# Hash attention and a maxout FFN on one core: order of the first hash, units of the values' parts, distance of the v loads, unit of one scaling, and two banks for the last product

## The chip, the cores and the metric

The kernel runs on one core of one Trainium2 chip. The metric is the device time of the whole program in microseconds (us). Three runs of the kernel before gave 295.3, 296.67 and 298.35 us; the median is 296.67 us. One execution was profiled, and all profile lines come from it.

## The reference

For 4 batches and 8 heads, `q`, `k` and `v` have 768 rows of 64 numbers. Each row of `q` and of `k` is projected on 6 directions, and the 6 signs give a bucket number. A query sees only the keys of its own bucket:

```
mask   = q_bucket[:, :, :, None] == k_bucket[:, :, None, :]
scores = 0.125 * q @ k.T ;  scores = where(mask, scores, -1e9)
attn   = softmax(scores) ;  a = attn @ v
x      = a.transpose(0, 2, 1, 3).reshape(3072, 512)
h      = max(x @ w1, x @ w2, x @ w3)          # w1..w3: 512 x 768
out    = h @ w_out                            # w_out: 768 x 512
```

Inputs and output are float32.

## The kernel before, in words

**Pairs and units.** The work is cut into 16 pairs of heads (4 per batch). A pair has 12 units: two query halves of 384 columns, times three pairs of key blocks, times two heads. So there are 192 units, 48 per batch, and u = 12 * pair + place. In this text "unit n" is the pass of the main loop (L408) with u = n, and its "slot" is u % 6. The scores of unit u+1 are issued in the pass of unit u.

**One unit.** `scores(u)` (L296) makes two matmuls of 384 columns into a double bank `sc` (two such buffers), and ScalarE takes the exponential of all 768 columns into one of 14 tiles `AT` (L304). The 70 rows that are contracted are 64 of the head and 6 of the hash, at +0.5 or -0.5, so that equal buckets add up to a constant that the bias takes away again; unequal buckets fall far below and vanish in the exponential.

**Values.** `values_part` (L316) multiplies the AT tiles of two units with the values `vo` into the bank `av`, four products side by side on 32 columns of the array each, and with ones into `sm`, the row sums. A query half has three parts. The last part comes in the pass after the half's last unit, in `values` (L336), where VectorE also moves `av` and `sm` out as `avs` and `ys` (L343 to L346). There is one `av` bank, so the first part of the next half needs `avs` to be done. The first two parts lie in slots 2 and 4 (L441). Pair 0's first half and pair 1's first half get all three parts at once.

**Preparation.** For each pair `prep_groups` (L133) yields four transposes groups `tgroup` (L143: three transposes into a bank `mp` of the pool `ms`, then VectorE copies to `T2` and, for pairs 2 to 7, to the odd half of `S`) and one `hashes` (L200: four float32 products side by side, VectorE turns them into `bits`, and four small DMAs put the bits into `S`). `even` (L216) is a GpSimd copy into `S`. One of these is issued in each "fill" slot: 1, 3 and 5 until unit 60, then 1 and 4 (L432). Preparation runs up to 6 pairs ahead. The pool `ms` has three banks; it also serves `sm`, the hash and the FFN.

**The start.** Pair 0 goes by a list written out by hand (L223 to L230). In it k and q of head 0 and k of head 1 are transposed first (L226), then the hash of head 0 runs (`hash_first`, L181: per head and side two float32 products, one per query or key half `par`, in different 32 columns), then q of head 1 is transposed. `bits_first` (L194) writes the signs straight into `S`, in pieces of (side, par, columns). For the first half of pair 0 and pair 1 the units of head 0 come ahead of those of head 1 (L284), so unit 3 is the first that needs head 1.

**Normalising.** `normalize` (L352) sends `ys` by DMA to 32 rows (`dd`), VectorE adds and inverts them (`rr`), a DMA writes them to DRAM (`rd`), and two DMAs spread them over 64 rows each (`rb`). GpSimd then multiplies `avs` and `rb` into `xT` (L381). A batch's last pair does that for each query half with the steps 7, 11 and 15 units after the half's end (L386); the others once per pair.

**FFN.** The groups of batch b-1 (L234) join the stream from place 13 of batch b on, so the first is due at unit 61 (`FFN_AT`, L291). They take turns with the units by a credit of 0.66 per unit. A first layer group is four matmuls of 384 columns, the fourth of which reads what the batch's last pair gave. A second layer product is six matmuls of 512 columns into one bank; ScalarE copies it out and a DMA of the sync queue stores it. The very last one is copied half by ScalarE and half by VectorE (L268 to L272).

**Queues.** All order is the order of the source (`manual_schedule`, L390): each engine works off its own list in order. GpSimd's list holds the casts of v (L125), the even copies, the scalings and also the issuing of nearly all loads: q and k (L115), v (L122), weights (L418) and bits (L214). `load_v` for pair p+1 is issued at the first unit of pair p (L411), its cast at place 10 (L415). The sync queue issues `dd`, `rd`, `rb` and the output.

Of the kernel before, what the change touches and what calls it, by code (L numbers as in the profile page):

```python
# [9 lines left out]
FP32 = mybir.dt.float32  # L10
# [7 lines left out]
def kernel(  # L18
# [114 lines left out]
    def prep_groups(pi):  # L133
# [34 lines left out]
                        nc.vector.tensor_copy(o, i_)  # L168
            return go

        def odd_first(hd):
            for side in (1, 0):
                o, i_ = st["S"][0:D, side, hd, 1, :], st["T2"][D : 2 * D, side, hd, :]
                if hd == 0:
                    nc.scalar.copy(o, i_)
                else:
                    nc.vector.tensor_copy(o, i_)

        first_bp = {}

        def hash_first(hd, sides=(1, 0)):  # L181
            for side in sides:
                if hd == 1:
                    bp = ms_ps.tile([P, 512], FP32, tag="ms", name="bp")
                elif side == 1:
                    bp = sc_ps.tile([P, 2, 512], FP32, tag="sc", name="bp0")[:, 0]
                else:
                    bp = av_ps.tile([P, 512], FP32, tag="av", name="bp1")
                first_bp[side, hd] = bp
                for par in range(2):  # L190
                    nc.tensor.matmul(bp[32 * par : 32 * par + 32, 0:HALF], pj[:, 1 + par, :], st["T2"][:, side, hd, :],  # L191
                                     start=True, stop=True)

        def bits_first(hd, parts):  # L194
            for side, par, lo, hi in parts:
                nc.vector.tensor_scalar(out=st["S"][D:KR, side, hd, par, lo:hi],
                                        in0=first_bp[side, hd][32 * par : 32 * par + NBITS, lo:hi],
                                        scalar1=0.0, scalar2=0.5, op0=AluOp.is_gt, op1=AluOp.subtract)
# [22 lines left out]
            return lambda: copy(st["S"][0:D, side, :, 1, :], st["T2"][D : 2 * D, side])  # L221

        if pi == 0:  # L223
            k0, k1 = (1, 0, 0, P), (1, 1, 0, P)
            early = (k0, k1, (0, 0, 0, HALF), (1, 0, P, HALF), (1, 1, P, HALF))
            return [tgroup(1, 0), tgroup(0, 0), tgroup(1, 1), lambda: odd_first(0), lambda: hash_first(0), tgroup(0, 1),  # L226
                    lambda: bits_first(0, early), lambda: scores(0), lambda: hash_first(1, (1,)), lambda: odd_first(1),
                    lambda: bits_first(1, early[:2]), lambda: scores(1), lambda: scores(2), lambda: hash_first(1, (0,)),
                    lambda: bits_first(1, early[2:]), lambda: bits_first(0, ((0, 1, 0, HALF),)),
                    lambda: bits_first(1, ((0, 1, 0, HALF),))]  # L230
        odds = [odd(1), odd(0)]
        return [tgroup(s, h) for h in (0, 1) for s in (1, 0)], hashes, [even], odds if pi == ODD_LATE or pi >= ODD_PSUM else []

    def ffn_groups(b):  # L234
        xb = xts[b]
        gs = []
        for hf in range(2):
            hts = {}
            for fb in range(NFB):
                for wi in range(3):  # L240
                    def go(fb=fb, wi=wi, hf=hf, hts=hts):
                        ps = ms_ps.tile([P, 512], FP32, tag="ms", name="l1")
                        for jc in range(NJC):
                            nc.tensor.matmul(ps[:, 0:HALF], w_sb[wi][:, jc, fb * P : (fb + 1) * P],  # L244
                                             xb[:, jc, hf * HALF : (hf + 1) * HALF],
                                             start=(jc == 0), stop=(jc == NJC - 1))
                        if wi == 0:
                            hts[fb] = hpool.tile([P, HALF], FP16, tag="ht", name="ht")
                            nc.vector.tensor_copy(hts[fb][:], ps[:, 0:HALF])  # L249
                        else:  # L250
                            nc.vector.tensor_tensor(out=hts[fb][:], in0=hts[fb][:], in1=ps[:, 0:HALF], op=AluOp.max)  # L251
                    gs.append((0.66, go, 0))
            for tb in range(CH2):
                st2 = {}

                def part(f0, f1, tb=tb, hts=hts, st2=st2):
                    if f0 == 0:
                        st2["l2"] = ms_ps.tile([P, 512], FP32, tag="ms", name="l2")
                    for fb in range(f0, f1):
                        nc.tensor.matmul(st2["l2"][:, 0:DM], hts[fb][:, tb * P : (tb + 1) * P], wout_sb[:, fb, :],  # L260
                                         start=(fb == 0), stop=(fb == NFB - 1))
                    return st2["l2"]

                def go2(tb=tb, hf=hf, part=part):
                    ps = part(NFB // 2, NFB)
                    osb = opool.tile([P, DM], FP32, tag="osb", name="osb")
                    rows = out[b * S : (b + 1) * S, :].rearrange("(p c) m -> p c m", c=NCH)
                    if (b, hf, tb) == (B - 1, 1, CH2 - 1):  # L268
                        nc.scalar.copy(osb[:, 0 : DM // 2], ps[:, 0 : DM // 2])
                        nc.vector.tensor_copy(osb[:, DM // 2 :], ps[:, DM // 2 : DM])  # L270
                        nc.scalar.dma_start(rows[:, 2 * tb + hf, 0 : DM // 2], osb[:, 0 : DM // 2])
                        nc.sync.dma_start(rows[:, 2 * tb + hf, DM // 2 :], osb[:, DM // 2 :])  # L272
                    else:
                        nc.scalar.copy(osb[:], ps[:, 0:DM])  # L274
                        nc.sync.dma_start(rows[:, 2 * tb + hf, :], osb[:])
                gs += [(0.66, lambda part=part: part(0, NFB // 2), 0), (0.66, go2, 0)]
        return gs


# [72 lines left out]
    def normalize(pi, q0, nq):  # L352

        b, jj = divmod(pi, HPAIR)
        if jj == 0:
            xts[b] = xpool.tile([P, NJC, S], FP16, tag="xT", name="xT")
        xt, avs, ys = xts[b], avs_of[pi], ys_of[pi]
        G = 16
        W = nq * HALF // G
        dd = small.tile([2 * G, 2, 2 * HALF // G], FP32, tag="dd", name="dd")  # L360
        rr = small.tile([2 * G, 2 * HALF // G], FP32, tag="rr", name="rr")
        rd = drp.tile([2 * G, W], FP32, tag=f"rd{nq}", name="rd")
        rb = rbpool.tile([P, 2, HALF], FP32, tag="rb", name="rb")

        def gather():
            for half in range(2):
                nc.sync.dma_start(dd[:, half, 0:W], ys[32 * half : P : D, q0 : q0 + nq, :])

        def invert():
            nc.vector.tensor_reduce(rr[:, 0:W], dd[:, :, 0:W].rearrange("p h w -> p w h"), axis=mybir.AxisListType.X,  # L370
                                    op=AluOp.add)
            nc.vector.reciprocal(rr[:, 0:W], rr[:, 0:W])  # L372
            nc.sync.dma_start(rd[:, :], rr[:, 0:W])

        def spread():
            for hd in range(2):
                nc.sync.dma_start(rb[hd * D : (hd + 1) * D, 0:nq, :],
                                    rd[hd * G : (hd + 1) * G, :].rearrange("(o p) i -> o (p i)", o=1).to_broadcast((D, nq * HALF)))

        def scale(i):  # L380
            return lambda: nc.gpsimd.tensor_mul(xt[:, jj, (q0 + i) * HALF : (q0 + i + 1) * HALF],  # L381
                                                avs[:, q0 + i, :], rb[:, i, :])
# [113 lines left out]
```

## Time and profile before

| what | value |
|---|---|
| median of three runs | 296.67 us (295.3 to 298.35) |
| the profiled execution's own time | 295.93 us |
| its span, first to last instruction | 294.0 us |
| granted TensorE clock, mean | 0.998 |
| TensorE busy (matmul) | 285.0 us, 97% |
| VectorE, ScalarE, GpSimd busy | 188.7, 195.4, 139.7 us |
| start of the first exponential | 9.08 us |
| first FFN group's last matmul starts | 71.05 us |
| end of the last matmul | 290.07 us |

The span is 1.93 us shorter than the time of the same execution; that rest lies outside of the instructions. Busy shares of TensorE hide short waits, since a matmul's row lasts until its result has left the array and so overlaps the next one. The starts of the rows, and their distance, tell more than the shares.

### The profile page before, as it was taken

The page shows a single profiled execution, that of the slowest core. Times are in us where ns is not written, and L with a number is a line of the kernel's source. Part 1 is how long each engine was busy: PE and PEld are TensorE (multiplying, and loading weights), DVE is VectorE, ACT ScalarE, POOL GpSimd, SP SyncE. Part 2 cuts the span into 40 slices and gives each one's busy share as a digit, 9 for nine tenths or more (in the row PEclk, how much of TensorE's full clock was granted, in tenths as well). Part 3 has the DMA queues.
Part 4 walks back from the last instruction along what each step waited for, and adds up shares of the span by engine and source line. Part 5 has one row for each costly group of instructions (what it writes and reads, how often), then busy time and mean ns, then how long its engine had stood idle before and what let it go on. Part 6 is the DMA issues. An engine that isn't in the chain of part 4 may idle for free.

```text
span 294.0 us, 6792 instructions
## 1 busy us (share of the span) xinstructions
PE 285.0 (97%) x2592; PEld 159.7 (54%) x2592; DVE 188.7 (64%) x419; ACT 195.4 (66%) x238; POOL 139.7 (48%) x187
## 2 busy tenths in 40 slices
PE   8898999998999999999999999999999999999994
PEld 4454454444656566555665556555655555555551
DVE  2886977788865387736667377654757167657480
ACT  3779899886847956797785965888696956010202
POOL 2765799889806556291905636090801702220000
PEclk9999999999999999999999999999999999999999
DMA  6877666864952733336222522315011211230203
GB/s 206 266 166 204 164 169 186 233 161 123 271 158 63 233 97 116 107 67 261 83 88 64 176 107 59 101 48 175 9 54 59 102 49 41 64 134 2 107 0 108
DMA packets 20276, 35.90 MB, mean 122 GB/s; under 512 B 6080, under 2 KB 12484, under 8 KB 20244
## 3 DMA queue, kind: packets, MB, share of 16 engines
q0 software_dynamic: 8992, 19.81, 25.2%
q1 hardware_dynamic: 10948, 15.52, 16.3%
q8 instruction: 20, 0.33, 0.5%
q10 hardware_dynamic: 304, 0.13, 0.2%
q14 instruction: 12, 0.10, 0.1%
HBM read 31.46 MB, written 6.39 MB: 129 GB/s over the span
## 4 chain that ended last, share of the span: by engine, by line
PE 90%; DMA 3%; DVE 2%; ACT 2%; issue 1%; POOL 0%; SPq 0%; ACTq 0%; POOLq 0%; DVEq 0%
PE l L244 32%; PE sc L301 21%; PE av L327 11%; PE l L260 11%; PE mp L150 6%; PE sm L332 5%; PE bp L205 3%; DMA rb<-rd 2%; ACT AT L304 2%; PE wm L393 1%; PE bp L191 1%; DMA rd<-rr 0%; DVE S L168 0%; POOL xT L381 0%; DVE rr L372 0%
## 5 line engine op out<-in xcount | busy, mean ns | idle before, releaser
L304 ACT ACTIVATE AT<-sc,bias_t 128x768 f16<-128x768 f32 x192 | 168.9, 903 | 53.9 <-PE sc L301 48.3
L244 PE MATMUL l<-xT,w_sb 128*128 128x384 f16 x576 | 110.0, 326 | 1.0 <-POOL xT L381 1.0
L301 PE MATMUL sc<-S 70*128 70x384 bf16 x384 | 93.8, 327 | 1.8 <-ACT AT L304 1.5
L244 PEld LDWEIGHTS <-w_sb 128*128 128x128 f16 x576 | 55.9, 97 | 36.3 <-issue 1.5
L214 POOL DMA_DIRECT2D S<-bits x58 | 32.9, 570 | 86.0 <-DVE bits L208 55.5
L251 DVE TENSOR_TENSOR ht<-ht,l 128x384 f16<-128x384 f16 x96 | 52.9, 551 | 18.1 <-PE l L244 13.5
L301 PEld LDWEIGHTS <-S 70*128 70x128 bf16 x384 | 33.8, 98 | 41.7 <-issue 20.2
L327 PE MATMUL av<-AT,vo 128*32 128x385 f16 x768 | 48.3, 330 | 1.0 <-DVE avs L344 0.7
L381 POOL TENSOR_TENSOR xT<-avs,rb 128x384 f16<-128x384 f32 x32 | 31.5, 1000 | 31.1 <-DMA rb<-rd 31.1
L249 DVE CAST ht<-l 128x384 f16<-128x384 f32 x48 | 26.5, 553 | 25.3 <-PE l L244 24.4
L274 ACT COPY osb<-l 128x512 f32<-128x512 f32 x23 | 13.4, 585 | 35.0 <-PE l L260 35.0
L260 PE MATMUL l<-wout_sb,ht 128*128 128x512 f16 x144 | 36.5, 379 | 0.0
L332 PE MATMUL sm<-AT,ones 128*32 128x384 f16 x384 | 32.7, 324 | 0.0
L327 PEld LDWEIGHTS <-vo 128*32 128x32 f16 x768 | 17.3, 95 | 20.0 <-issue 10.9
L160 DVE COPY T<-mp 128x384 f32<-128x384 f32 x31 | 17.0, 549 | 13.7 <-PE mp L150 13.6
L158 DVE TENSOR_SCALAR T<-mp 128x384 f32<-128x384 f32 x30 | 16.6, 554 | 12.7 <-PE mp L150 11.3
L217 POOL CAST S<-T 64x1536 bf16<-64x1536 f32 x15 | 22.1, 1476 | 0.0
L260 PEld LDWEIGHTS <-ht 128*128 128x128 f16 x144 | 14.0, 97 | 12.7 <-DVE ht L251 0.2
L344 DVE TENSOR_SCALAR avs<-av,sv 128x384 f32<-128x384 f32 x32 | 19.8, 618 | 1.6
L346 DVE TENSOR_SCALAR ys<-sm 128x384 f32<-128x384 f32 x32 | 17.5, 548 | 0.0
L343 DVE TENSOR_SCALAR sv<-av 128x1 f32<-128x1 f32 x32 | 5.1, 158 | 18.3 <-PE av L327 17.8
L150 PE MATMUL mp<-iden,knat 128*128 128x128 f32 x96 | 16.2, 277 | 0.0
(45 smaller groups left out, 191.4 us busy)
## 6 DMA issues: line engine op xcount, KB each, us to landing
out_dram<-osb SPq DMA_DIRECT2D x23, 256.0 KB
vnat<-in_v_dram POOLq DMA_DIRECT2D x15, 384.0 KB, 4.8
knat<-in_k_dram POOLq DMA_DIRECT2D x13, 384.0 KB, 4.3
qnat<-in_q_dram POOLq DMA_DIRECT2D x13, 384.0 KB, 5.1
rb<-rd SPq DMA_DIRECT2D x24, 192.0 KB
w_sb<-in_moe_w_dram POOLq DMA_DIRECT2D x12, 192.0 KB, 4.7
rb<-rd SPq DMA_DIRECT2D x16, 96.0 KB
S<-bits POOLq DMA_DIRECT2D x58, 9.0 KB, 2.4
```

Of the source, the lines that this page charges most:

```text
L150: nc.tensor.transpose(mp[:, i * P : (i + 1) * P], n[:, hd, 2 * i * D : (2 * i + 2) * D], iden[:])
L214: eng.dma_start(st["S"][D:KR, side, hd, :, :], bits[p0 : p0 + 2 * NBITS, :])
L217: nc.gpsimd.tensor_copy(st["S"][0:D, :, :, 0, :], st["T2"][0:D])
L244: nc.tensor.matmul(ps[:, 0:HALF], w_sb[wi][:, jc, fb * P : (fb + 1) * P], xb[:, jc, hf * HALF : (hf + 1) * HALF], start=(jc == 0), stop=(j ...
L249: nc.vector.tensor_copy(hts[fb][:], ps[:, 0:HALF])
L251: nc.vector.tensor_tensor(out=hts[fb][:], in0=hts[fb][:], in1=ps[:, 0:HALF], op=AluOp.max)
L260: nc.tensor.matmul(st2["l2"][:, 0:DM], hts[fb][:, tb * P : (tb + 1) * P], wout_sb[:, fb, :], start=(fb == 0), stop=(fb == NFB - 1))
L301: nc.tensor.matmul(sc[:, j, 0:HALF], th[0:KR, 1, hd, j, kp * P : (kp + 1) * P], th[0:KR, 0, hd, qh, :], start=True, stop=True)
L304: nc.scalar.activation(at[:, :, 0:HALF], sc[:, :, 0:HALF], ActFn.Exp, bias=bias_t[:], scale=SCALE)
L327: nc.tensor.matmul(av[p0 : p0 + 32, 0 : HALF + 1], vones[pi][:, hd, d0 : d0 + 32], ats[hd][:, c % 2, 0 : HALF + 1], start=(c == 0), stop=( ...
L332: nc.tensor.matmul(sm[32 * t : 32 * t + 32, 0:HALF], ones[:, :], ats[hd][:, half, 0:HALF], start=(s == 0), stop=(s == CH2 - 1))
L381: return lambda: nc.gpsimd.tensor_mul(xt[:, jj, (q0 + i) * HALF : (q0 + i + 1) * HALF], avs[:, q0 + i, :], rb[:, i, :])
```

## The change

It has five parts.

1. **The first hash in pieces.** `odd_first` and `hash_first` take single sides and single pieces. Head 0's list is now: transposes of k and q; the products of k's first 128 columns (both halves), of q's first half; their bits; the products of k's other 256 columns; transposes of head 1's k; scores 0; head 1's k products; then transposes of head 1's q; scores 1; the product of head 1's first q half; scores 2; and last the products of the second q halves of both heads, one by one.
2. **Parts and fills.** Until unit 60 the fills are in slots 1, 2 and 4 and the values' parts in slots 3 and 5 (the third stays in slot 0).
3. **v.** Pair p+2's v is loaded from place 8 of pair p on (pair 1's from unit 0), and cast at place 4 of the pair before its own (pair 1's at unit 10 still).
4. **Scaling.** The scaling of a batch's last pair, except the very last pair, comes 14 units after a half's end in place of 15.
5. **The last product** is computed in two halves of 256 columns, each with six matmuls into a bank of its own. VectorE copies the first and the sync queue stores it, ScalarE copies the second and its own queue stores it. It is one FFN item instead of two.

```
-        def odd_first(hd):
+        def odd_first(hd, side):
+            copy = nc.scalar.copy if hd == 0 else nc.vector.tensor_copy
+            copy(st["S"][0:D, side, hd, 1, :], st["T2"][D : 2 * D, side, hd, :])
...
+        def hash_first(hd, parts):
+            for side, par, lo, hi in parts:
+                if (side, hd) not in first_bp:
...
+                nc.tensor.matmul(first_bp[side, hd][32 * par : 32 * par + 32, lo:hi], pj[:, 1 + par, :],
+                                 st["T2"][:, side, hd, lo:hi], start=True, stop=True)
...
-            k0, k1 = (1, 0, 0, P), (1, 1, 0, P)
-            early = (k0, k1, (0, 0, 0, HALF), (1, 0, P, HALF), (1, 1, P, HALF))
-            return [tgroup(1, 0), tgroup(0, 0), tgroup(1, 1), lambda: odd_first(0), lambda: hash_first(0), tgroup(0, 1),
...
+            ka, kb = [[(1, par, lo, hi) for par in range(2)] for lo, hi in ((0, P), (P, HALF))]
+            qa, qb = [[(0, par, 0, HALF)] for par in range(2)]
+            hf, bf = hash_first, bits_first
+            return [tgroup(1, 0), tgroup(0, 0), lambda: odd_first(0, 1), lambda: odd_first(0, 0),
+                    lambda: hf(0, ka), lambda: hf(0, qa), lambda: bf(0, ka), lambda: bf(0, qa),
+                    lambda: hf(0, kb), tgroup(1, 1), lambda: bf(0, kb), lambda: scores(0),
+                    lambda: hf(1, ka + kb), lambda: odd_first(1, 1), lambda: bf(1, ka), tgroup(0, 1),
+                    lambda: scores(1), lambda: hf(1, qa), lambda: odd_first(1, 0), lambda: bf(1, qa), lambda: scores(2),
+                    lambda: bf(1, kb), lambda: hf(1, qb), lambda: hf(0, qb), lambda: bf(0, qb), lambda: bf(1, qb)]
...
+                    if last:
+                        for c0, copy, eng in ((0, nc.vector.tensor_copy, nc.sync), (DM // 2, nc.scalar.copy, nc.scalar)):
+                            cs = slice(c0, c0 + DM // 2)
+                            ps = part(0, NFB, cs.start, cs.stop)
+                            copy(osb[:, cs], ps[:, 0 : DM // 2])
+                            eng.dma_start(rows[:, 2 * tb + hf, cs], osb[:, cs])
...
-            return [(4, invert), (6, spread), (8, scale(0))] if pi == NPAIR - 1 else [(7, invert), (11, spread), (15, scale(0))]
+            return [(4, invert), (6, spread), (8, scale(0))] if pi == NPAIR - 1 else [(7, invert), (11, spread), (14, scale(0))]
...
-            if u % UPP == 0 and pi + 1 < NPAIR:
-                cast_v[pi + 1] = load_v(pi + 1, nc.gpsimd)
+            ahead = 1 if u == 0 else 2 if u % UPP == 8 else NPAIR
+            if pi + ahead < NPAIR:
+                cast_v[pi + ahead] = load_v(pi + ahead, nc.gpsimd)
...
-            if u % UPP == 10 and pi + 1 < NPAIR:
+            if u % UPP == (4 if pi else 10) and pi + 1 < NPAIR:
...
-                fill = slot in (1, 3, 5) if u < UPB + FFN_AT else slot in (1, 4)
+                fill = slot in (1, 2, 4) if u < UPB + FFN_AT else slot in (1, 4)
...
-            if slot in (2, 4) and UPG < u < PAIRS_AT and u // UPG != 2:
+            if slot in (3, 5) and UPG < u < PAIRS_AT and u // UPG != 2:
```

More of the change, by code (lines that the diff above doesn't have):

```diff
@@ L169, in tgroup @@
             return go
-        def odd_first(hd):
[L172 to L177, printed above, removed]
-        first_bp = {}
[L181 to L192, printed above, removed]
+        def odd_first(hd, side):
+            copy = nc.scalar.copy if hd == 0 else nc.vector.tensor_copy
+            copy(st["S"][0:D, side, hd, 1, :], st["T2"][D : 2 * D, side, hd, :])
+        first_bp = {}
+        def hash_first(hd, parts):
+            for side, par, lo, hi in parts:
+                if (side, hd) not in first_bp:
+                    if hd == 1:
+                        bp = ms_ps.tile([P, 512], FP32, tag="ms", name="bp")
+                    elif side == 1:
+                        bp = sc_ps.tile([P, 2, 512], FP32, tag="sc", name="bp0")[:, 0]
+                    else:
+                        bp = av_ps.tile([P, 512], FP32, tag="av", name="bp1")
+                    first_bp[side, hd] = bp
+                nc.tensor.matmul(first_bp[side, hd][32 * par : 32 * par + 32, lo:hi], pj[:, 1 + par, :],
+                                 st["T2"][:, side, hd, lo:hi], start=True, stop=True)
         def bits_first(hd, parts):
@@ L223, in prep_groups @@
         if pi == 0:
-            k0, k1 = (1, 0, 0, P), (1, 1, 0, P)
-            early = (k0, k1, (0, 0, 0, HALF), (1, 0, P, HALF), (1, 1, P, HALF))
-            return [tgroup(1, 0), tgroup(0, 0), tgroup(1, 1), lambda: odd_first(0), lambda: hash_first(0), tgroup(0, 1),
[L227 to L230, printed above, removed]
+            ka, kb = [[(1, par, lo, hi) for par in range(2)] for lo, hi in ((0, P), (P, HALF))]
[7 more added lines that the diff above has]
+                    lambda: bf(1, kb), lambda: hf(1, qb), lambda: hf(0, qb), lambda: bf(0, qb), lambda: bf(1, qb)]
         odds = [odd(1), odd(0)]
@@ L254, in ffn_groups, with part @@
                 st2 = {}
-                def part(f0, f1, tb=tb, hts=hts, st2=st2):
+                last = (b, hf, tb) == (B - 1, 1, CH2 - 1)
+                def part(f0, f1, c0=0, c1=DM, tb=tb, hts=hts, st2=st2):
                     if f0 == 0:
@@ L259, in part, with go2 @@
                     for fb in range(f0, f1):
-                        nc.tensor.matmul(st2["l2"][:, 0:DM], hts[fb][:, tb * P : (tb + 1) * P], wout_sb[:, fb, :],
-                                         start=(fb == 0), stop=(fb == NFB - 1))
+                        nc.tensor.matmul(st2["l2"][:, 0 : c1 - c0], hts[fb][:, tb * P : (tb + 1) * P],
+                                         wout_sb[:, fb, c0:c1], start=(fb == 0), stop=(fb == NFB - 1))
                     return st2["l2"]
-                def go2(tb=tb, hf=hf, part=part):
-                    ps = part(NFB // 2, NFB)
+                def go2(tb=tb, hf=hf, part=part, last=last):
                     osb = opool.tile([P, DM], FP32, tag="osb", name="osb")
                     rows = out[b * S : (b + 1) * S, :].rearrange("(p c) m -> p c m", c=NCH)
[L268 to L272, printed above, removed]
+                    if last:
[4 more added lines that the diff above has]
+                            eng.dma_start(rows[:, 2 * tb + hf, cs], osb[:, cs])
                     else:
+                        ps = part(NFB // 2, NFB)
                         nc.scalar.copy(osb[:], ps[:, 0:DM])
                         nc.sync.dma_start(rows[:, 2 * tb + hf, :], osb[:])
-                gs += [(0.66, lambda part=part: part(0, NFB // 2), 0), (0.66, go2, 0)]
+                gs += ([] if last else [(0.66, lambda part=part: part(0, NFB // 2), 0)]) + [(0.66, go2, 0)]
         return gs
```

## The prediction

> **What bounds the kernel now.** I read the page first. TensorE is busy almost throughout, so what counts is where its rows stand apart.
>
> ```profile
> PE 285.0 (97%) x2592; PEld 159.7 (54%) x2592; DVE 188.7 (64%) x419; ACT 195.4 (66%) x238; POOL 139.7 (48%) x187
> ```
>
> Second, the chain of waits, between 35 and 75 us. Columns: start, length, what.
>
> ```profile
> 38.79 0.43 PE sc L301 x2
> 39.22 0.33 PE mp L150 x3
> 39.55 0.33 PE sc L301 x2
> 39.88 0.44 PE av L327 x8
> 40.32 0.16 PE sm L332 x4
> ...
> 52.46 0.63 DVE avs L344
> ...
> 62.59 7.28 DMA rb<-rd
> ```
>
> Two units take 1.69 us, all TensorE: scores 0.33 us, a transposes group 0.33, a values' part 0.60, and 0.10 more for the scores behind a part. So a unit with a fill is "light" (0.66) and one with a part "heavy" (1.03). ScalarE would need only 0.79 per exponential. From unit 8 to 61 TensorE sets the pace wherever nothing makes it wait. The table of waits, 40 to 84 us, shows what does (total, times, longest):
>
> ```profile
> PEld L327 <- DVE avs L344: 1.5, 2, 1.1
> PE l L244 <- POOL xT L381: 1.0, 1, 1.0
> PEld L327 <- POOL vo L125: 0.7, 1, 0.7
> ```
>
> A half's first part waits for VectorE to empty the one `av` bank, once for GpSimd's cast of v; the first FFN group waits for the first scaling of pair 3, on GpSimd:
>
> ```profile
> 62.46 0.72 POOL L122 DMA_DIRECT2D vnat<-in_v_dram  x1
> ...
> 66.03 2.30 POOL L214 DMA_DIRECT2D S<-bits  x4 [0.86 <-DVE bits L208]
> 68.33 1.48 POOL L217 CAST S<-T 64x1536 bf16<-64x1536 f32 x1
> 70.01 0.99 POOL L381 TENSOR_TENSOR xT<-avs,rb 128x384 f16<-128x384 f32 x1 [0.21 <-DMA rb<-rd]
> ```
>
> Its last input `rb` landed at 69.87 and GpSimd was free at 69.81: both bind. From 73 us on, units come in steps of 0.98 and 1.31 us (four FFN matmuls 0.65, scores 0.33, a transposes group 0.33) without gaps. So what the first FFN group gains or loses goes to the end one to one.
>
> Third, the start, TensorE's and ScalarE's timelines:
>
> ```profile
> 6.33 1.48 PE L191 MATMUL bp<-T,pj 128*32 128x384 f32 x8
> ...
> 8.97 0.84 PE L191 MATMUL bp<-T,pj 128*32 128x384 f32 x4
> ...
> 12.04 0.48 PE L301 MATMUL sc<-S 70*128 70x384 bf16 x2 [0.70 <-ACT AT L304]
> ```
> ```profile
> 9.08 0.90 ACT L304 ACTIVATE AT<-sc,bias_t 128x768 f16<-128x768 f32 x1 [0.26 <-PE sc L301]
> 10.28 1.69 ACT L304 ACTIVATE AT<-sc,bias_t 128x768 f16<-128x768 f32 x2 [0.30 <-PE sc L301]
> 12.56 4.07 ACT L304 ACTIVATE AT<-sc,bias_t 128x768 f16<-128x768 f32 x5 [0.58 <-PE sc L301]
> ```
>
> Each of the hash's products leaves two rows. Four products take 1.48 us, two take 0.84, so a side's two products, which write different rows of a bank, take 0.64 us together. Exponentials 0, 1 and 3 start at 9.08, 10.28 and 12.56. Last, the tail:
>
> ```profile
> 290.15 0.37 ACT L269 COPY osb<-l 128x256 f32<-128x256 f32 x1 [0.71 <-PE l L260]
> 290.55 0.42 DVE L270 COPY osb<-l 128x256 f32<-128x256 f32 x1 [3.76 <-ACT osb L269]
> 291.01 0.33 SPq L272 DMA_DIRECT2D out_dram<-osb  x1
> ```
>
> The second copy starts only when the first has ended, though they read different columns of the bank.
>
> **Part 1, the first hash.** Removed: two paired runs (0.64 each) for the query sides. Added: three lone ones. A product alone lasts as long as a pair, since both stream 384 columns (bounds: 0, if it runs beside a neighbour, and 0.64; I take 0.64, as all but the first share rows with their neighbour or stand between scores). Step by step: `T2` of head 0's k is there at 6.02, of q at 6.59, as now. qa runs 6.68 to 7.32 and is seen at 7.49; its bits (0.55) are done at 8.09, scores 0 start at 8.24. Exponential 0 then waits for ScalarE's copy of head 1's k until 8.9: it starts at 8.81, 0.27 earlier. But head 1's k is transposed only behind qa and kb, 7.85 to 8.18 (now 5.86 to 6.24), copied by 8.91, hashed 9.00 to 9.64; then q is transposed 9.74 to 10.07, copied by ScalarE by 10.81 (now 8.82). ScalarE makes that copy ahead of exponential 1, which starts at 10.71: 0.43 later. Scores 2 stand behind qa of head 1 (10.90 to 11.54): exponential 2 at 12.07 against 11.08. Then come the two lone second halves, 1.28 us, 11.87 to 13.16, and behind them scores 3, now at 12.04: 1.1 later. The first of the two also writes the bank that VectorE reads for head 1's first bits until 12.3. By the tail's two copies I take it that a bank's user waits for the other: 0.55 more (bounds 0 and 0.55). VectorE then ends these bits about as much later, and the copies for pair 1, its hash and the first three parts stand behind them, as they do now from 13.69 to 18.02. Sum +1.65 us at unit 8 (bounds -0.3, if all lone products are hidden and the first exponential's gain stays, and +1.7).
>
> The Trainium skill, "PSUM — Partial Sum Buffer", section on bank collisions, says that engines must be kept apart by bank and quadrant of 32 rows, by bank alone being the simple version. The second halves go to rows 32 and up, the bits are read from row 0, so by the fine rule that wait falls away and my forecast would be 0.55 lower; the tail's copies cover all rows and cannot tell the two apart.
>
> **Part 2, parts and fills, units 8 to 61.** Removed: the waits of first parts. The rows show 0.74 (unit 44), 0.37 (unit 50, the cast of v), 0.15 and 0.11 (units 10, 32): -1.37. With a unit more between, `avs` (done 1.1 us after the half's last product, rows at 40.48 and 41.56) is in time. Added: two light units in a row, slots 1 and 2. The third scores need the buffer of the first, which is free 0.59 + 0.90 + 0.05 = 1.54 us after its scores began, TensorE is there after 1.32: about 0.2, five times (units 7, 19, 31, 37, 49) where both fills are transposes: +1.0, of which ScalarE's slack at unit 7 may take some; I take 0.8. Second, the hash. Fills counted off, hashes fall to units 14, 25, 34, 44, 55 (now 15, 25, 35, 45, 55), and in 14, 34 and 44 the last transposes are one or two units back, with VectorE still at the closing copies (0.16 + 0.62 + 0.55) and the copies of the groups before (1.14 each). At 44: VectorE copies the last group at 53.45 now; a fill moved up brings that to 52.6, ready at 53.2, while TensorE is there at 52.3: 0.85 us. At 34: the copy cannot be earlier than now, 43.72 to 44.28, TensorE is ready at 43.3: 0.8. At 14: ready at 25.0 against 24.2, but ScalarE paces there: 0.4. Sum: +2.05 + 0.8 - 1.37, about +1.4 (bounds -1.4, if VectorE is never late, and +4.3, below). No DMA of the sync queue moves with this; the loads of q and k, which the first group issues on GpSimd (0.74 + 0.73), move by a unit.
>
> **Parts 3 and 4, v and the scaling.** In front of the scaling at 70.01 GpSimd loses the even copy (1.48, now behind it) and v 5's issue (0.72, now issued at unit 44), and gains the cast of v 5 (0.83) and v 6's issue (0.72). The cast fits into the 0.86 idle ahead of 66.03. So it is free at 66.03 + 2.30 + 0.72 = 69.05 and done at 70.05; with its bits read off VectorE up to 0.2 earlier, 69.85. `rb` now has q, k and a weight of 0.94 MB ahead of it rather than 1.32 MB; at some 200 GB/s in these slices that is 1.9 us, so it lands near 68. TensorE arrives at 69.92. All this stands on unit 55's hash, so it shifts with the units, and the wait is gone: -1.1 (bounds -1.1 and 0). Elsewhere the moved issues and casts lie in a queue that is busy 45.76 of 53.0 us; the cover is that bits and copies are for pairs at least one pair ahead. From 73 us on TensorE has no gap to win.
>
> **Part 5, the tail.** Before, ScalarE's copy, then VectorE's (0.42), then an issue at 291.01. Now VectorE's copy and the sync queue's issue lie beside the second half's matmuls, and ScalarE's issue, at 290.55 now, is last: -0.46; twelve matmuls of 256 columns for six of 512 stream the same, but each needs its weights (98 ns) within 108 ns: +0.06. -0.4 (bounds -0.5 and +0.1).
>
> **Sum.** 1.65 + 1.4 - 1.1 - 0.4 = +1.55. Against the profiled execution's 295.93 us (span 294.0 and 1.93 outside): 297.5. That execution stood 0.74 under the median of 296.67, so for a median I say 298.2.
>
> **Rivals.**
> - *VectorE becomes the bound of stage one (slower).* At 30 to 50 us it is busy 16.64 of 20.00. Slots 0 to 2 now give it the closing copies and two groups, 1.3 + 2.3 us, in TensorE's 2.35; it is 1.25 late, and the group in slot 4 then waits for a bank of `ms`, 0.2, or 0.95 where an inverse (0.74) is in the queue. At 0.55 per half over nine halves that is 5.0 rather than the 2.05 taken: +2.9, 301.1. It decides from about 0.4 per half up. Against it: over 12 units VectorE's work is unchanged and some 9 of 10 us.
> - *Everything fits (faster).* Lone products are hidden, hashes find their inputs: -0.3 - 1.4 - 1.1 - 0.4 = -3.2, 293.5. For it: the three waits are real. Against: scores 3 behind 1.28 us of products.
> - *The wait for xT stays.* If `rb` is no earlier against the units, or GpSimd's added issue and cast are not covered: +1.1, 299.3.
>
> **How the numbers follow.** About 1% (2.97 us) is what a measurement of this kernel can tell from no change: the runs spread over 3 us. Forecast 0.40, xT's wait stays 0.13 (0.08 of it within 1%, 0.05 over), VectorE's bound 0.30, everything fits 0.17. So faster 0.17, same 0.48, slower 0.35. The forecast's own range is 296.3 to 299.6; over all cases 293.9 to 301.2, which cuts the far ends of the second and first rival.
>
> **What would show it.** Exponential 0 near 8.8 but 3 near 13.7 to 14.2, and 8 near 20 rather than 18.56, bear out part 1. Hashes at L205 that wait for VectorE at three places, no `av` row that waits for `avs`, and scores 62 about 3 us later bear out part 2. No wait of L244 for `xT`, and the last issue within 0.5 us of the last matmul, bear out the rest. It is wrong if exponential 3 starts before 12.6, or if the step from unit 8 to 62 (50.75 us now) gets shorter.

## The result and the profile after

Nine runs of each kernel: after 298.42 us median (298.04 to 299.52), before 296.23 us (295.3 to 298.35). The ratio is 1.0076, with a 95% interval of 1.0051 to 1.0101: slower by 0.8%, inside the 1% that was called "same". Forecast was 298.2 us.

The profiled execution of after took 299.52 us (span 297.6), 1.10 over its median; that of before took 295.93 (span 294.0), 0.30 under its median. So the two traces stand 3.6 us apart, the medians 2.19. The traces tell where time went; how much of it a typical run pays is told by the ratios. (In two of the experiments, the paired products and the hashes three units behind, the granted clock of the profiled execution fell after 60 us, to 0.99 over the whole run; of these only earlier rows are used.)

Columns: start of the scores of a unit, in us.

| unit | before | after | difference |
|---|---|---|---|
| 0 | 8.56 | 8.40 | -0.16 |
| 3 | 12.04 | 13.92 | +1.88 |
| 8 | 18.02 | 19.92 | +1.90 |
| 12 | 21.56 | 24.07 | +2.52 |
| 62 | 68.77 | 72.89 | +4.13 |
| 63 | 72.51 | 75.96 | +3.45 |
| 191 | 248.28 | 251.75 | +3.47 |
| end of the span | 294.0 | 297.6 | +3.6 |

The time is lost in three stretches (start, unit 12, units 13 to 62), 0.7 us comes back at unit 63, and from there to the end nothing changes. The page's line of busy times, by itself, does not show the loss as idle time:

```profile
PE 289.3 (97%) x2606; PEld 160.9 (54%) x2606; DVE 189.2 (64%) x419; ACT 195.8 (66%) x238; POOL 140.2 (47%) x187
```

VectorE, ScalarE and GpSimd are busy as before to within 0.5 us. TensorE's busy time grew by 4.3 us with only 14 instructions more. Two things are in it: the query's hash products no longer run side by side, and rows run through waits, as the hash rows further down show. So the starts of the rows tell where the time went, and the busy time does not.

The start, TensorE's and ScalarE's timelines of after:

```profile
8.40 0.49 PE L301 MATMUL sc<-S 70*128 70x384 bf16 x2
...
11.80 0.50 PE L301 MATMUL sc<-S 70*128 70x384 bf16 x2
12.51 1.48 PE L187 MATMUL bp<-T,pj 128*32 128x384 f32 x4 [0.21 <-DVE S L192]
13.92 0.50 PE L301 MATMUL sc<-S 70*128 70x384 bf16 x2
```
```profile
9.11 0.90 ACT L304 ACTIVATE AT<-sc,bias_t 128x768 f16<-128x768 f32 x1
10.49 0.49 ACT L154 ACTIVATE T<-mp 128x384 f32<-128x384 f32 x1 [0.48 <-PE mp L150]
10.88 0.90 ACT L304 ACTIVATE AT<-sc,bias_t 128x768 f16<-128x768 f32 x1
12.34 0.90 ACT L304 ACTIVATE AT<-sc,bias_t 128x768 f16<-128x768 f32 x1 [0.56 <-PE sc L301]
14.46 4.07 ACT L304 ACTIVATE AT<-sc,bias_t 128x768 f16<-128x768 f32 x5 [1.21 <-PE sc L301]
```

Two lone products (four rows, 1.48 us) stand between scores 2 and scores 3, and ScalarE waits 1.21 us for them. The table of waits of after, 18 to 76 us, holds what replaced the waits shown of before:

```profile
PEld bp L201 <- DVE T L158: 1.5, 3, 0.5
...
PE sc L301 <- DMA S<-bits: 0.8, 1, 0.8
PE sc L301 <- ACT AT L304: 0.7, 2, 0.4
...
PE l L242 <- DVE S L168: 0.3, 1, 0.3
```

No `av` row waits for `avs`, none for the cast of v, and no FFN group for `xT`. In their place the hash waits for VectorE's copies at three units, scores 12 wait for a DMA, and an FFN group waits for VectorE. The hash rows of the two kernels, first before, then after, show the same thing: 1.01, 0.85 and 0.85 us became 1.51, 1.40 and 1.51.

```profile
25.21 1.01 PE L205 MATMUL bp<-T,pj 128*32 128x384 f32 x8
...
44.39 0.85 PE L205 MATMUL bp<-T,pj 128*32 128x384 f32 x8
...
54.16 0.85 PE L205 MATMUL bp<-T,pj 128*32 128x384 f32 x8
```
```profile
27.22 1.51 PE L201 MATMUL bp<-T,pj 128*32 128x384 f32 x8
...
46.95 1.40 PE L201 MATMUL bp<-T,pj 128*32 128x384 f32 x8
...
56.74 1.51 PE L201 MATMUL bp<-T,pj 128*32 128x384 f32 x8
```

GpSimd around the first scaling of pair 3, and the first FFN groups (at 73.56 in after):

```profile
69.76 2.28 POOL L210 DMA_DIRECT2D S<-bits  x4 [1.48 <-DVE bits L204]
72.03 0.75 POOL L122 DMA_DIRECT2D vnat<-in_v_dram  x1
72.80 1.02 POOL L381 TENSOR_TENSOR xT<-avs,rb 128x384 f16<-128x384 f32 x1
73.74 1.48 POOL L213 CAST S<-T 64x1536 bf16<-64x1536 f32 x1
```
```profile
72.89 0.50 PE L301 MATMUL sc<-S 70*128 70x384 bf16 x2
73.23 0.49 PE L150 MATMUL mp<-iden,knat 128*128 128x128 f32 x3
73.56 1.46 PE L242 MATMUL l<-xT,w_sb 128*128 128x384 f16 x8
75.31 0.81 PE L242 MATMUL l<-xT,w_sb 128*128 128x384 f16 x4 [0.29 <-DVE S L168]
75.96 0.49 PE L301 MATMUL sc<-S 70*128 70x384 bf16 x2
```

The scaling starts right behind the issue of v, as forecast, with nothing to wait for, and is in time. But unit 61 hands TensorE three FFN groups at once, and the third waits for a bank of `ms` that VectorE has not read yet: it starts 0.45 us behind its turn. The tail, from ScalarE's, VectorE's and the sync queue's timelines:

```profile
293.63 0.37 ACT L270 COPY osb<-l 128x256 f32<-128x256 f32 x1 [0.72 <-PE l L259]
294.04 0.35 ACTq L271 DMA_DIRECT2D out_dram<-osb  x1
```
```profile
292.99 0.42 DVE L270 COPY osb<-l 128x256 f32<-128x256 f32 x1 [2.73 <-ACT osb L274]
```
```profile
293.71 0.33 SPq L271 DMA_DIRECT2D out_dram<-osb  x1
```

The last issue is at 294.04, 0.49 behind the end of the last matmul (293.55); before it was 0.94 behind (291.01 against 290.07). Yet from the start of scores 191 to the end of the span it takes 45.88 us, before 45.74.

### The profile page after: what moved, and what is told of

Same layout as the page of the kernel before. It is cut to its first block, busy times and chain, and to the rows that moved or that the text cites. A ratio compares the mean times of both kernels' runs of the same rounds, so it can differ in the third digit from the quotient of the medians.

```text
span 297.6 us, 6817 instructions
## 1 busy us (share of the span) xinstructions
PE 289.3 (97%) x2606; PEld 160.9 (54%) x2606; DVE 189.2 (64%) x419; ACT 195.8 (66%) x238; POOL 140.2 (47%) x187
## 4 chain that ended last, share of the span: by engine, by line
PE 92%; DMA 3%; ACT 2%; DVE 1%; issue 1%; ACTq 0%; SPq 0%
PE l L242 31%; PE sc L301 22%; PE av L327 12%; PE l L259 10%; PE mp L150 6%; PE sm L332 5%; PE bp L201 4%; PE bp L187 2%; ACT AT L304 2%; DMA pst<-in_proj_dram 1%; DMA S<-bits 1%; DVE T L160 0%; DVE avs L344 0%; DVE S L168 0%; ACTq L89 0%
## 5 line engine op out<-in xcount | busy, mean ns | idle before, releaser
L259 PE MATMUL l<-wout_sb,ht 128*128 128x512 f16 (+1 forms) x150 | 36.5, 370 | 0.0
L213 POOL CAST S<-T 64x1536 bf16<-64x1536 f32 x15 | 22.2, 1477 | 0.0
L259 PEld LDWEIGHTS <-ht 128*128 128x128 f16 x150 | 14.6, 97 | 12.3 <-DVE ht L249 0.2
```

The costliest lines, as they stand in the source:

```text
L213: nc.gpsimd.tensor_copy(st["S"][0:D, :, :, 0, :], st["T2"][0:D])
L259: nc.tensor.matmul(st2["l2"][:, 0 : c1 - c0], hts[fb][:, tb * P : (tb + 1) * P], wout_sb[:, fb, c0:c1], start=(fb == 0), stop=(fb == NFB - 1))
```

## The experiments

Each kernel ran beside the kernel before on the same chip. Ratios are to those runs (medians 296.03 to 296.16), with 95% intervals. "Unit n +x" is the start of its scores in the profiled execution against that of before.

### The parts alone

The edits are the parts of the diff above, one by one. First part 1, the first hash.

> Kernel before with the new first hash alone. Theory (the start's delay reaches the end in full): scores of unit 3 start 1.6 to 1.9 us later than before's 12.04, scores of unit 8 as much later, the wait of the first FFN group for xT stays near 1.0 us because its inputs hang on the same units, and the time is 1.5 to 1.9 us longer. Rival (the delay is taken up by that wait): the FFN starts only 0.5 us later and the time is at most 0.6 us longer.

Measured: 297.75 us, 1.0071 [1.0051, 1.0090]. Unit 3 +1.64, unit 8 +1.65, unit 12 +2.45. So in this execution the order of the start costs what the forecast gave it, and a wait of 0.9 us for the landing of pair 1's bits comes on top at unit 12, which the forecast does not have.

Part 2, parts and fills.

> Kernel before with the new slots of fills and parts alone. Theory: no values row waits for avs any more (1.4 us less), but two light units in a row cost about 0.15 each five times, and the hashes of units 14, 34 and 44 wait 0.4 to 0.9 us each for VectorE: the step from the scores of unit 8 to those of unit 62 grows from 50.74 to about 52 us, time 1 to 1.5 us longer. Rival (the hash waits come from the delayed start or the moved v, not from the slots): the step shrinks to about 49.5 us and the time is 1 us shorter.

Measured: 300.14 us, 1.0158 [1.0126, 1.0191]. Unit 46 +1.54, unit 53 +2.48, unit 63 +3.35. The direction holds, the size does not (1 to 1.5 us were expected, the medians give 4.0): without part 3 a first part meets the cast of pair 4's v, and the FFN waits 1.8 us for `xT`. The row of the former:

```profile
62.28 0.51 PE L327 MATMUL av<-AT,vo 128*32 128x385 f16 x8 [1.20 <-POOL vo L125]
```

Parts 3 and 4, v and the scaling.

> Kernel before with v two pairs ahead and the scaling at 14 alone. Theory: the wait for xT (1.0 to 1.1 us) and the one for the cast of v at unit 50 (0.37) go, time 1.0 to 1.5 us shorter. Rival (the landing of rb is set by other traffic, or GpSimd's added issue and cast take the gain): rb lands no earlier against the units and the time changes by less than 0.4 us.

Measured: 295.56 us, 0.9985 [0.9972, 0.9999]: a gain of 0.5, not 1.1. The step from unit 51 to 52 fell only from 1.40 to 1.30 us: the first part no longer waits for the cast of v there, but still 0.27 us, for VectorE. The step from unit 62 to 63, which takes 2.61 without any wait (scores 0.33, transposes 0.33, three groups of 0.65), takes 3.44. The timelines of TensorE and GpSimd have:

```profile
69.11 1.81 PE L244 MATMUL l<-xT,w_sb 128*128 128x384 f16 x8
71.24 0.81 PE L244 MATMUL l<-xT,w_sb 128*128 128x384 f16 x4 [0.32 <-DVE S L168]
```
```profile
68.77 1.02 POOL L381 TENSOR_TENSOR xT<-avs,rb 128x384 f16<-128x384 f32 x1
```

Eight matmuls take 1.81 us, in after 1.46. By the single matmuls of the trace the fourth, which needs `xT`, starts 0.24 us behind its turn, 0.05 us after the scaling has ended: so the wait for `xT` shrank from 1.13 us to 0.24 and did not go. The third group then waits 0.48 us for a bank of `ms` that VectorE has not read. In after, where TensorE comes to this place later, the first of these waits is gone and the second is 0.45. With the scaling at 15 and the old places of parts and fills, the wait for `xT` differs between executions: 0.88 to 1.63 us in six of them, 1.13 in before.

Part 5, the tail.

> Kernel before with the last product in two banks alone. Theory: the last issue stands about 0.4 us closer to the last matmul, and the time is 0.3 to 0.5 us shorter. Rival (what ends the program is the landing of the last store, which takes longer from ScalarE's queue): no more than 0.1 us shorter, or longer.

Measured: 295.9 us, 1.0010 [0.9994, 1.0026]: nothing gained.

Parts 2, 3 and 4 together, that is the changed kernel without its first hash and its tail:

> The changed kernel without its first hash and without its tail: values' parts and fills at the new places, v two pairs ahead, the scaling at 14. Theory (the new places alone cost what the forecast said, 1.4 us up to unit 62, by late hashes; what they cost beyond that without the early v, 3.4 us, was the exposed cast of v and xT): scores 62 1.2 to 1.8 us later than before, three hashes with steps near 1.8 us, no wait for the cast of v, the step from 62 to 63 3.06 us: 296.7 to 297.3. Rival (the late hashes come from the late start, which leaves VectorE behind): hashes in units 14, 34 and 44 take 1.2 to 1.4 us, and the time is at or under 296.0.

Measured: 297.03 us, 1.0029 [1.0014, 1.0044]. Unit 8 -0.55 (its first inputs landed earlier), unit 62 +0.85: the new places cost 1.40 us between these units. In after it is 2.23, of which 0.8 is the wait at unit 12. The three late hashes are there without the late start (first, third and fourth hash):

```profile
23.80 1.51 PE L205 MATMUL bp<-T,pj 128*32 128x384 f32 x8
...
43.53 1.39 PE L205 MATMUL bp<-T,pj 128*32 128x384 f32 x8
...
53.32 1.66 PE L205 MATMUL bp<-T,pj 128*32 128x384 f32 x8
```

So they come from the slots and not from the start. The step from 62 to 63 is 3.06, as in after.

### What the first hash loses by

The query's two products side by side again, transposes at the change's places:

```
-  hf(0, qa) ... hf(1, qa) ... hf(1, qb), hf(0, qb)
+  hf(0, qa + qb) ... hf(1, qa + qb)
```

> The kernel before with the new first hash alone, but with the query's two products side by side again (both written one behind the other, first and second half together, for head 0 and for head 1); head 1's transposes stay at their new, late places. Theory (the loss of 1.64 us at scores 3 comes from two lone products of 0.64 us at the end, the first of which also waits for VectorE's bank): no row waits for the bits near 12.5, scores 3 start near 12.6 to 12.9, 1.1 to 1.3 us earlier than with the new first hash; about 0.5 us of the loss stays, from the late transposes and from scores 0 behind a pair. The wait of scores 12 for the landing of pair 1's bits (0.9 us) stays in whole or grows, because ScalarE's copy of head 1's q, and behind it the loads on GpSimd, are still late. Time: 296.5 to 297.0 against 296.1 before. Rival (the late transposes cost it all): scores 3 at 13.3 or later and the time as with the new first hash, 297.7.

Measured: 296.92 us, 1.0041 [1.0021, 1.0061]; unit 3 +0.24, unit 8 +0.28, unit 12 +1.20. So the lone products, with the first one's wait for VectorE, cost 1.4 of the 1.64 us. In TensorE's timeline scores 3 follow scores 2 without them:

```profile
11.51 0.50 PE L317 MATMUL sc<-S 70*128 70x384 bf16 x2
12.28 0.48 PE L317 MATMUL sc<-S 70*128 70x384 bf16 x2 [0.27 <-issue]
```

The wait of unit 12 stays. For it, head 1's transposes back at their early places, the lone products kept:

```
-  tgroup(0, 0), ... hf(0, kb), tgroup(1, 1), ... bf(1, ka), tgroup(0, 1)
+  tgroup(0, 0), tgroup(1, 1), ... hf(0, qa), tgroup(0, 1), ... hf(0, kb)
```

> The kernel before with the new first hash alone, but with head 1's transposes back at their early places (k's ahead of the hash of head 0, q's behind qa); the lone products stay where the change puts them. Theory (two causes, lone products at unit 3 and late copies of head 1 for GpSimd's loads at unit 12): scores 3 still near 13.2 to 13.7 (1.1 to 1.6 us later than before), but the loads of pair 3's q and k on GpSimd are issued at about 11.7 as before rather than at 13.9, and scores 12 wait no longer for the landing of the bits: the loss at unit 12 equals that at unit 3. Time: 296.9 to 297.4. Rival (the wait at unit 12 comes from VectorE's late bits, not from GpSimd's loads): the wait of about 0.9 us at unit 12 stays although the loads are early.

Measured: 297.85 us, 1.0065 [1.0050, 1.0079]; unit 3 +1.26, unit 12 +1.13, no wait for the bits. The loads that were late with part 1 alone (first fence) are early again (second). Scores 12 read the bits of pair 1's head 0; these go by the sync queue and not by GpSimd's (L213 of the kernel before), and each fence ends with their row from the sync queue's timeline:

```profile
13.69 0.71 POOL L115 DMA_DIRECT2D knat<-in_k_dram  x1
14.40 0.72 POOL L115 DMA_DIRECT2D qnat<-in_q_dram  x1
...
18.91 1.80 SPq L210 DMA_DIRECT2D S<-bits  x2
```
```profile
11.56 0.71 POOL L115 DMA_DIRECT2D knat<-in_k_dram  x1
12.27 0.72 POOL L115 DMA_DIRECT2D qnat<-in_q_dram  x1
...
18.53 1.78 SPq L210 DMA_DIRECT2D S<-bits  x2
```

From the end of this issue to scores 12 it is 3.30 us in the first, 0.88 of it waiting, and 2.37 in the second, without a wait. In the trace's DMA records the bits' last packet ends 1.91 us behind the end of the issue in the first and 0.80 in the second. VectorE's bits were late in both (the issue is at 17.26 in before), so the rival falls: the bits land late where GpSimd's loads are late. In the first the last of the loads ahead, a weight, landed 1.05 us after the bits had been issued, in the second 0.71 us before. That the two hold each other up on the DMA engines is the likely reason and no more: in the kernel with parts 2 to 4 the bits took 0.80 us too, with loads still under way. The size varies as well: the five profiled executions with late loads wait 0.29 to 1.34 us at unit 12, those with early loads 0.08 at most. The loads were issued later because GpSimd's copy for pair 0 waits for ScalarE's copy of head 1's q, which part 1 had moved. The time did not follow the trace, though (297.85 where 296.9 to 297.4 was expected): 0.5 us went into a longer wait for the cast of v ahead of scores 52 (that step is 1.92 rather than 1.40 us).

The two lone products in the other order, so that the first writes a bank that nobody reads:

```
-  hf(1, qb), hf(0, qb), bf(0, qb)
+  hf(0, qb), hf(1, qb), bf(0, qb)
```

> The kernel before with the new first hash alone, and with the two lone second halves in the other order: head 0's, whose bank nobody reads at that time, ahead of head 1's, whose bank VectorE is reading. Theory (a product waits while VectorE reads other rows of its bank): the first lone product starts right behind scores 2, 0.2 to 0.4 us earlier, no row of L187 waits for VectorE there, and scores 3 start 0.2 to 0.4 us earlier, near 13.3 to 13.5. Rival (it waits for the bits themselves, or the row's wait is covered by something else): scores 3 near 13.7, as with the order of the change.

Measured (one run): 298.01 us. From scores 2 to scores 3 it takes 1.84 rather than 2.12 us, and the row has lost its wait:

```profile
11.65 0.50 PE L299 MATMUL sc<-S 70*128 70x384 bf16 x2
12.08 1.48 PE L187 MATMUL bp<-T,pj 128*32 128x384 f32 x4
```

So in this kernel a product to rows 32 and up does wait while VectorE reads row 0 and up of the same bank; it costs 0.28 us. The Trainium skill, "PSUM — Partial Sum Buffer", "PSUM bank collisions raise a hardware error", gives bank and quadrant as the rule and bank alone as the simple version. The wait seen here does not spare another quadrant. Whether it goes by bank or by tile this run cannot tell, since head 1's two query products write one tile in one bank.

### Hashes three units behind their transposes

`ready_at` notes the unit of a pair's last transposes plus 3; the rest is the changed kernel.

```
-  if hash_ready and u < PAIRS_AT:
+  if hash_ready and u < PAIRS_AT and (u <= UPG or u >= ready_at[-1]):
```

> The changed kernel, but a pair's hash is written only when its last transposes lie three units or more back; the rest is the same. Theory (hashes in units 14, 34 and 44 find VectorE's copies late, 0.5 to 0.65 us each): their steps fall from 1.8 us to about 1.2 us, the three waits of weight loads for T go, and the step from unit 8 to 62 gets 1.0 to 1.8 us shorter than in the changed kernel; time 296.8 to 297.5 against 298.4. Rival (VectorE is the bound of this stage): the waits come back one or two units later, at another group or at the scores, and the time stays within 0.5 us of 298.4.

Measured: 1.0086 [1.0061, 1.0111], not seen to differ from after; the fastest run took 297.79 us, after's fastest 298.04. The profiled execution took 303.91 us. Between units 0 and 46 it wins 2.1 us on after (one hash, 0.5, is still to come), then VectorE waits in its queue for a pair's sums, and a first part waits for VectorE:

```profile
57.40 0.24 DVE L370 TENSOR_REDUCE rr<-dd 32x48 f32<-32x96 f32 x1 [3.74 <-DMA dd<-ys]
```
```profile
59.01 0.51 PE L327 MATMUL av<-AT,vo 128*32 128x385 f16 x8 [2.58 <-DVE avs L344]
```

So the theory holds up to unit 46: the late hashes can be had without their waits. In this execution the gain was then lost one place later, to a DMA's landing at the head of VectorE's queue. The ratio is as the rival has it, but not for its reason: here VectorE stood idle and was not the bound. Whether the shorter runs have this wait stays open, and with it what the order is worth.

### One FFN group at unit 61

The kernel with parts 3 and 4 alone, and:

```
-  f_credit = min(f_credit + 0.66, 1.4)
+  f_credit = min(f_credit + 0.66, 0.66)
```

> The kernel before with v loaded two pairs ahead and the first scaling at 14, and with the credit for FFN groups capped at one group (0.66 rather than 1.4), so that unit 61 gives one FFN group and not three. Theory (v and scaling gained 0.5 us rather than 1.1 because the second and third group of unit 61 wait for a bank of ms, 0.3 to 0.5 us each time, which VectorE empties late): no row of L244 waits for VectorE between 69 and 72 us, nothing waits for xT, and 0.3 to 0.6 us come on top: 294.9 to 295.3 us against 295.5 to 295.6 with v and scaling alone and 296.0 before. Rival (the groups only move, and the wait comes back at the next groups, since TensorE has the same work to do and VectorE the same to empty): 295.5 to 295.8.

Measured: 294.88 us, 0.9968 [0.9950, 0.9986]. It is faster than both kernels. Its interval overlaps that of parts 3 and 4 alone (0.9972 to 0.9999), so the gain on those is read from the traces. TensorE's and GpSimd's timelines:

```profile
69.03 1.06 PE L244 MATMUL l<-xT,w_sb 128*128 128x384 f16 x4
69.94 0.49 PE L301 MATMUL sc<-S 70*128 70x384 bf16 x2
70.26 0.81 PE L244 MATMUL l<-xT,w_sb 128*128 128x384 f16 x4
```
```profile
68.70 1.02 POOL L381 TENSOR_TENSOR xT<-avs,rb 128x384 f16<-128x384 f32 x1
```

Scores 63 start 1.94 us ahead of the kernel without the cap. Two groups of 0.65 were only put off, and they come back at the end (from scores 191 on, 47.07 rather than 45.75 us); the other 0.6 is gone for good. The theory holds for VectorE: no group waits for a bank at this place any more. It does not hold for `xT`: the first group takes 1.06 instead of 0.81 us, because its fourth matmul again waits 0.25 us, until the scaling has ended at 69.72.

### The tail

What the trace's DMA records show in every kernel here is a packet of 8192 bytes on queue 14, named "instruction", which takes some 0.3 to 0.55 us near the last store. In us:

```
kernel              last issue       8192-byte packet   last completion   issue's end to completion
before              291.01-291.34    291.13-291.49      292.39            1.05
new tail alone      289.83-290.18    290.44-290.86      291.66            1.48
after               294.04-294.39    294.66-295.06      295.86            1.47
```

Behind the new tail both stores' packets are in flight when it comes, and of each store's 16 completions one is 0.4 us later than the rest, as if one of the 16 DMA engines had been taken. Over all profiled executions the last column is 1.03 to 1.09 us in the nine with the old tail, where no completion stands apart, and 1.33 to 1.48 in the five with the product in two banks. In the nine the packet begins about 0.13 us behind the start of the last issue, or, in the kernel with the capped credit, only when the stores are landing. To see whose packet it is, both halves were stored by the sync queue:

```
-  (DM // 2, nc.scalar.copy, nc.scalar)
+  (DM // 2, nc.scalar.copy, nc.sync)
```

> The kernel before with the new tail alone, but both halves of the last product are stored by the sync queue, the second behind ScalarE's copy; nothing is issued on ScalarE's queue. Theory (the 8 KB packet of queue 14 belongs to ScalarE's issue, about 0.25 us behind it, and holds one of the 16 DMA engines for 0.4 us while the stores' packets are on it): the packet goes to another time, both stores land 1.1 us after their issue, and the span's end behind the last matmul falls from 4.2 to 3.8 us: 295.4 to 295.7 against 296.0. Rival (the packet belongs to the program's end and falls between the last issue and its landing whatever the queue): it comes again between the last issue and the landing, one packet of the store lands 0.4 us late, and the time is that of before within 0.2 us.

Measured: 1.0000 [0.9986, 1.0015]. The packet came at 291.59 to 291.93, behind the last issue's end at 291.47; the last completion at 292.80 was 0.31 us later than the one ahead of it. The rival holds: the packet does not hang on ScalarE's queue. The Trainium skill, "Runtime: NRT & Kernel Launch", "Instruction fetch mechanics", says that a sequencer fetches its next block of instructions over a DMA queue of its own; the queue's name agrees. What sets the moment is open, and no run has the new tail without the packet inside the store, so that the packet is the whole reason is argued and not shown.

### An order with all that seemed good

Part 1 with early transposes and paired query products, parts 3 and 4, and the new tail with its two queues exchanged; fills and parts as before.

> The kernel before with the parts of the change that gain or should gain: v loaded two pairs ahead and the first scaling at 14; the first hash in pieces, but with early transposes and with the query's two products side by side; the last product in two banks with the queues exchanged (the first half by ScalarE and its queue, the second by VectorE and the sync queue); values' parts and fills at the old places. Theory: scores 3 0.5 to 0.9 us earlier than before, nothing lost at unit 12, 0.5 us from v and scaling, 0 to 0.4 from the tail: 294.4 to 295.2 us. Rival (the order of the start is bound by VectorE's bits and by the copies of head 1, however the pieces are ordered): the start gains nothing and the time is that of v and scaling alone, 295.5.

Measured: 296.42 us, 1.0015 [1.0001, 1.0030], no gain. Scores 0 came 0.71 us later than before. In this order all of head 0's products, k's last ones too, are written ahead of the bits, and VectorE starts on the bits only behind them:

```profile
7.96 1.94 DVE L192 TENSOR_SCALAR S<-bp 6x128 bf16<-6x128 f32 x5 [1.94 <-PE bp L187]
```
```profile
9.27 0.49 PE L319 MATMUL sc<-S 70*128 70x384 bf16 x2 [0.88 <-DVE S L192]
```

Unit 3 +1.21, unit 62 +1.02, unit 63 +0.71. The exchanged queues gained nothing either: from scores 191 to the end 45.76 us, with the packet at 291.85 to 292.25 and one completion 0.42 us behind the others. None of the five orders in pieces reached scores 3 as early as the list of before.

## Why the prediction was right, and where it was not

**Part 1: right by its steps, lucky in the hundredths.** +1.65 was forecast at unit 8 and +1.65 measured alone. The other two profiled executions with this start give +1.75 (hashes three units behind) and +1.90 (after, where the projection reached VectorE at 5.48 us and not at 5.24 as in the kernel with part 1 alone). The old start varies too: scores 8 came at 17.47 to 18.02 in seven executions, and before's is the latest of them. So the term holds to some 0.3 us. Alone, exponentials 0, 1 and 2 started at 8.86, 10.64 and 12.10 (forecast 8.81, 10.71, 12.07), scores 3 at 13.68 (forecast 12.04 + 1.65 = 13.69). Two terms behind it were mis-sized and cancel. Without the bank's wait the forecast has the lone second halves from 11.87 and scores 3 at 13.16; in the other order, which has no such wait, they came at 12.08 and 13.49, 0.33 later. The bank's wait was taken as 0.55 and is 0.28. Of the 1.65 the runs give 1.09 to the lone products, 0.28 to the bank, and 0.28 to the rest, which stays when the products are paired. (The forecast's opening count of three lone products is a slip: the list has four, and its step by step has all four.)

**Missed: the landing at unit 12.** The forecast followed part 1 to unit 8 and no further. That GpSimd's copy waits for head 1's q, and that the bits' landing is late when the loads behind this copy are late, was not costed: 0.8 us in after, 0.29 to 1.34 over the five executions with late loads. By the medians part 1 alone costs 1.66 us in all; how a typical run divides that between the start and this landing stays open.

**Part 2: right.** +1.4 forecast, +1.40 measured with the early v. In after's rows the steps of the three hash units are 1.86, 1.76 and 1.87 against 1.21 us for a hash without a wait, +1.85 where 2.05 stood (0.4, 0.8, 0.85 became 0.65, 0.55, 0.65). Two light units in a row cost 0.22 four times and 0.16 once, 1.04 where 0.8 stood. The first-part waits are gone (-1.37). These three add up to 1.52, and with the third hash of parts 2 to 4 alone (2.01) to 1.65; smaller differences elsewhere give the rest back, so the terms hold to 0.2 us and no closer. What the forecast did not say is that this sum needs part 3: without it the same places cost 3.4 us in the profiled execution and 4.0 by the medians.

**Parts 3 and 4: right mechanism, wrong size.** -1.1 became -0.7 in after's step from unit 62 to 63 and -0.5 alone. In after the wait for `xT` is gone, as forecast; alone 0.24 of it stays. The failed step is "what the first FFN group gains or loses goes to the end one to one": with the first group on time, the third waits 0.45 us (0.48 alone) for a bank of `ms`, which VectorE empties late. With the capped credit that wait is gone, and 0.6 us more is won.

**Part 5: wrong.** The last issue moved by 0.45 us as forecast, but -0.4 became 0 (ratio 1.0010 [0.9994, 1.0026]). The step that failed took the landing to be a fixed time behind the issue; it grew from 1.05 to 1.47 us.

**The rivals.** "VectorE becomes the bound" is not seen: 1.85 us at three hashes, not 5.0 over nine halves. "Everything fits" fell at scores 3. "The wait for xT stays" fell in after, though another wait at the same place took 0.45 of its 1.1. By the medians the parts add up to 1.66 + 0.87 + 0 = 2.5 where 1.55 was forecast and 2.19 measured. The two large terms held; parts 3 to 5 together were 0.8 too good. That 298.2 lies so near 298.42 is in part luck: it stood on the median of the first three runs of before, 296.67, where nine gave 296.23. The change itself was forecast 0.64 us too small.

**The signs.** Most came as named: three hashes wait for VectorE, no first part waits for `avs`, no L244 row for `xT`, the last issue is 0.49 us behind the last matmul. Exponential 0 came at 9.11 in after (8.8 was named), 3 at 14.46 (13.7 to 14.2), 8 at 20.45 (20), and scores 62 are 4.13 us later and not about 3: the landing at unit 12 and the later inputs make up most of that.

## What to carry to other kernels

When a wait at the head of a queue is taken away, look who needs what next, at the very same place: here a later FFN group needed a bank, and more of the gain was had when fewer groups came at once. Follow a moved copy through every queue behind it: a copy on ScalarE delayed a copy on GpSimd, that delayed loads, and with the late loads a small DMA of another queue landed late, 8 us on. And two narrow matmuls that ran side by side are only to be parted if something useful runs during each: here two pairs that became four lone products cost 1.09 us.

## What was not expected of the hardware

- In the five executions where a packet of 8192 bytes on an instruction queue (0.31 to 0.42 us long) falls into the last store's packets, one of that store's 16 completions comes 0.31 to 0.43 us behind the others. In the nine others none does.
- The start varies by up to 0.55 us between executions with the same code up to there: scores 0 at 8.56 in before and at 8.01 in the kernel with parts 2 to 4, with the first landings.
- Landings of small DMAs can decide more than their size says: scores waited 0.29 to 1.34 us for the bits when large loads of another queue had been issued some 2 us later, and 0.08 us at most otherwise.
